# RWKV attention with a squared-ReLU FFN: half of the w_in loads issued on the ACT queue, with new order tables

## The chip, the cores and the metric

The kernel runs on one core of one Trainium2 chip. The metric is the device time of one execution in microseconds. Before the change three runs took 559.23, 558.83 and 562.87 us; the median is 559.23 us.

## The reference

The inputs have 4 sequences (batch), 8 heads, 768 positions and a head width of 48. First a linear recurrence with decay runs over the positions, then a two-layer FFN with a squared ReLU runs over all 3072 tokens, with 384 inputs and 2048 hidden units. All is float32.

```python
for t in range(S):                       # per sequence and head
    kt, vt, rt, wt = (k[:, :, t], v[:, :, t], r[:, :, t], w[:, :, t])
    cur = np.einsum('bhd,bhe->bhde', u[None] * kt, vt)
    y[:, :, t] = np.einsum('bhd,bhde->bhe', rt, state + cur)
    state = wt[:, :, :, None] * state + np.einsum('bhd,bhe->bhde', kt, vt)
x = y.transpose(0, 2, 1, 3).reshape(B * S, H * D)
h = np.maximum(x @ w_in, 0.0)
out = h * h @ w_out
```

## The kernel before

The 768 positions are cut into 6 chunks of 128. A chunk of one sequence is a "unit", so there are 24 units, four to a chunk. The recurrence inside a unit is done by matmuls.

**One unit** goes through these steps. SP loads w, k and r into a tile `st` (one transfer each, for one or for two sequences) and v into `v`. For chunk 0 TensorE transposes them (`turn`, line 399); later chunks use VectorE's stream transpose and small transfers (`z`, `pt`). VectorE forms the running product of w (`scan`, line 411), ACT takes its logarithm and an exponential of minus that (`ln`, lines 418 and 419), VectorE makes the scaled r and k (`rt`, `kn`, lines 422 to 431), TensorE multiplies them (`mt`, line 459), ACT builds the diagonal term (`diag`, line 448, eight small instructions in a unit), VectorE masks (`mask`, line 463), TensorE mixes in v (`mix`, lines 484 to 508), and ACT and VectorE write the result as a high and a low part into `x` (lines 525 and 526). ACT also runs a range check on w (`far`, lines 450 and 451).

**The weights** come in 8 groups g. The loads of `w_in` go to a tile `ri`, those of `w_out` to `ro`. A group of `w_in` is four transfers: for the lower half of the partitions one of 48 rows (288 KB) and one of 16 rows (96 KB), and the same for the upper half (`load_w`, line 305). A group of `w_out` is one transfer of 768 KB (line 307). Each group is then split into a high and a low part (`split_w`): ACT (line 318), VectorE three times (322, 326, 331), ACT (338), GpSimd (339).

**The FFN** runs in steps f = 0 to 15 for each chunk: nine matmuls into `hp` (line 573), ReLU and square by ACT and VectorE (578 to 582), then three matmuls for each sequence into `ob` (line 588). For the first 6 steps of chunk 0 and for all of chunk 1 a step is done for two sequences at a time (256 columns instead of 512).

**The order** of everything is set by a planner inside the kernel (`Plan`). Each step is added with an engine, a cost and a rank. The planner repeatedly takes the step that can start earliest by its own costs and, among equals, the one of lowest rank. The ranks come from tables: `AT` and `AT0` by the name of the step, `U0`, `C1`, `W0`, `WL` by unit or weight group, `OFF` and `LAG` for the FFN. The planner has two transfer queues, `"sp"` and `"actq"`; it keeps for each queue a time of its own at which its wire is free. A step of `"actq"` takes its place in the instruction order of ACT.

**Landing semaphores.** The transfers of both queues are numbered in program order and take eight landing semaphores (DMAHW0 to DMAHW7) in turn. A transfer is issued only once the transfer eight places before it has landed; its engine's queue stands still until then. Before the change only the load of `u` at the start and the last four stores are on the ACT queue; everything else is on SP.

Of the kernel before, what the change touches and what calls it, by code (L numbers as in the profile page):

```python
# [169 lines left out]

@with_exitstack
def kernel(
    ctx: ExitStack,
# [37 lines left out]
    wi_r, wi_t, wo_r, wo_t = [], [], [], []  # L213
# [10 lines left out]
    for i in range(3):  # L224
        g = place(f"g{i}", [128, 2, 512], F32R, None)
# [11 lines left out]
    far = const.tile([128, NC * B], F32, name="far")  # L237
# [17 lines left out]
    P = Plan()  # L255
# [42 lines left out]
    def load_w(g, rank):  # L298
        before = first_use(0) if g == NG - 1 else [s for s in P.steps if any(x.pool == "ly" for x in s.slots)] if g == NG - 2 else []

        pairs = w_in32[g, 0:KT * R].rearrange("(k p) x -> p k x", k=KT)
        for j in range(2):
            last = w_in32[g, KT * R + j * D:KT * R + j * D + D].rearrange("(k p) x -> p k x", k=KT)
            for i, (to, n, src) in enumerate(((j * J, D, pairs[j * D:j * D + D]), (j * J + D, J - D, last))):
                P.add("sp", 1.4 if n == D else 0.5, rank, lambda to=to, n=n, src=src: nc.sync.dma_start(out=wi_r[g][to:to + n], in_=src),
                      w=[("wi", g, j, i)], after=before if g == NG - 1 else [], runs=3 * n)
        P.add("sp", 2.4, rank, lambda: nc.sync.dma_start(out=wo_r[g], in_=w_out32[g]), w=[("wo", g, 0, 0)],
              after=before, runs=256)

    def split_w(g, rank):  # L310
        for nm, rt, tt, parts in (("wi", wi_r[g], wi_t[g], [("wi", g, j, i) for j in range(2) for i in range(2)]),
                                  ("wo", wo_r[g], wo_t[g], [("wo", g, 0, 0)])):
            bits = rt.rearrange("p k x -> p (k x)").rearrange("p (x z) -> p x z", z=2)
            q = Slot("q")
            raw, lead = (nm, g, "raw"), (nm, g, "lead")

            def widen(q=q, bits=bits):
                A.activation(q.tile, bits.bitcast(F32)[:, :, 1], AF.Copy, scale=2.0 ** -112)

            def shift(q=q):  # L320
                qi = q.tile.bitcast(U32)
                V.tensor_scalar(out=qi, in0=qi, scalar1=3, scalar2=None, op0=ALU.logical_shift_left)

            def sign(q=q, bits=bits):
                qi = q.tile.bitcast(U32)
                V.scalar_tensor_tensor(out=qi, in0=bits[:, :, 1], scalar=0x80000000, in1=qi,
                                       op0=ALU.bitwise_and, op1=ALU.bitwise_or)

            def low(q=q, bits=bits):
                qi = q.tile.bitcast(U32)  # L330
                V.scalar_tensor_tensor(out=qi, in0=bits[:, :, 0], scalar=29, in1=qi,
                                       op0=ALU.logical_shift_right, op1=ALU.bitwise_or)

            P.add("act", 0.8, rank, widen, r=parts, w=[q])
            P.add("dve", 0.48, rank, shift, w=[q], port=True)
            P.add("dve", 0.88, rank, sign, r=parts, w=[q], port=True)
            P.add("dve", 0.88, rank, low, r=parts, w=[q], port=True)
            P.add("act", 0.74, rank, lambda q=q, tt=tt: A.copy(out=tt[:, 0], in_=q.tile), r=[q], w=parts + [lead])
            P.add("pool", 1.9, rank, lambda q=q, tt=tt: G.tensor_tensor(out=tt[:, 1], in0=q.tile, in1=tt[:, 0].bitcast(F32), op=ALU.subtract),
                  r=[q, lead], w=[(nm, g, "rest")])  # L340
# [221 lines left out]
    def ffn(P, c, f, rank, bs=(0, B), s0=None):  # L562
        n = (bs[1] - bs[0]) * C
        xT = xTs[c if c == SLOW else c % 2]
        xs = slice(bs[0] * C, bs[1] * C)
        hp, g = Slot("hp"), Slot("g")
        wkeys = lambda nm: [(nm, f // 2, "lead"), (nm, f // 2, "rest")]

        def first():
            m = 0  # L570
            for kt in range(KT):
                for wl, xl in ((0, 0), (0, 1), (1, 0)):
                    T.matmul(hp.tile[:, 0:n], wi[f][:, wl, kt], xT[:, kt, xl, xs], start=(m == 0), stop=(m == 3 * KT - 1))  # L573
# [7 lines left out]
        P.add("act", 0.53 if full else 0.31, rank("g"), lambda: A.copy(out=hi(), in_=h()), r=[hp], w=[(g, 0)])  # L581
        P.add("dve", 0.61 if full else 0.33, rank("g"), lambda: V.tensor_tensor(out=lo(), in0=h(), in1=hi().bitcast(F32), op=ALU.subtract),  # L582
              r=[hp, (g, 0)], w=[(g, 1)])
        for b in range(*bs):
            def second(b=b):
                for m, (gl, wl) in enumerate(((0, 0), (0, 1), (1, 0))):
                    o = (b - bs[0]) * C
                    T.matmul(obs[b][:, 0:DM], g.tile[0][:, gl, o:o + C], wo[f][:, wl], start=(f == 0 and m == 0), stop=(f == NF - 1 and m == 2))  # L588
            P.add("pe", 0.525, rank("ob"), second, r=wkeys("wo") + [(g, 0), (g, 1)], w=[("ob", b)])
            if f == NF - 1:  # L590
                os_ = Slot("q")
                ob = out[b * S:b * S + S]
                P.add("act", 0.4, rank("os"), lambda b=b, os_=os_: A.copy(out=os_.tile[:, 0:DM], in_=obs[b][:, 0:DM]), r=[("ob", b)], w=[os_])  # L593
                q_, e = ("actq", nc.scalar) if c == NC - 1 else ("sp", nc.sync)
                P.add(q_, 1.1, rank("os"), lambda b=b, os_=os_, ob=ob, e=e: e.dma_start(out=ob[c * C:c * C + C] if s0 is None else ob[ds(s0, C)], in_=os_.tile[:, 0:DM]), r=[os_])


    AT = {"load": -12.5, "z": -10, "pt": -10.5, "rk": -7.0, "beta": -5.0, "far": 9.25, "v": -6.0, "scan": -2.25, "ln": 7.0, "rt": -6, "kn": 3.25, "diag": -3.5, "mt": 5, "mask": 3.25, "ktp": 5.25, "kt": 12.5, "mix": 4.25, "x": 1.5, "x3": -5.0, "send": 3.0, "dS": 3.5, "S": 1.25}
    AT0 = {"load": -13.0, "turn": -1.5, "rk": -2, "beta": 0.2, "far": 9.25, "v": -6.75, "scan": -1.75, "ln": 5.25, "rt": 0.25, "kn": 2, "diag": 9.5, "mt": -1.0, "mask": 3.75, "ktp": 7.25, "kt": -1, "mix": 3, "x": 7.75, "x3": -1, "send": 4.0, "dS": 7.5, "S": -4}
    U0 = (-16, -15.25, -6.75, -5.5)  # L600
    C1 = (5.25, 13, 34.5, 36)
    WL = (-8.25, -8, -9, -5.5, -1.75, -7, -8.25, -13.5)
    OFF = {"hp": -1.0, "g": -6.5, "ob": 0.75, "os": -7.5}
    W0 = (-12.5, -9.5, -1, 0.25, 0.25, 5.5, 5.0, 17)
    HALF = (6, 16, 0, 0, 0, 0)
    LAG = 2

    def rank_of(c, b):
        if c == 0:
            return lambda nm: U0[b] + AT0[nm]  # L610
        return lambda nm: (C1[b] if c == 1 else 8 * ((c - 1) * B + b) - 4) + AT[nm]

    for b in range(B):
        attention(0, b, rank_of(0, b))
    for g in range(NG):
        load_w(g, W0[g] + WL[g])
        split_w(g, W0[g])
    x = 0
    for c in range(NC):
        if c:  # L620
            for b in range(B):
                attention(c, b, rank_of(c, b))

        order = [(f, bs) for bs in ((0, 2), (2, B)) for f in range(HALF[c])] + [(f, (0, B)) for f in range(HALF[c], NF)]
        for f, bs in order:
            step = (bs[1] - bs[0]) / 2
            ffn(P, c, f, lambda nm, x=x, step=step: x + OFF[nm] + (LAG * step if nm in ("ob", "os") else 0), bs)
            x += step
    with tc.manual_schedule():
        P.run()  # L630
# [14 lines left out]
    with tc.If(any_bad > 0):  # L645
        with tc.tile_pool(name="dram", bufs=1, space=bass.MemoryType.DRAM) as dr, \
# [8 lines left out]
            with tc.For_i(0, S, TB) as t0:  # L655
# [8 lines left out]
                for t in range(TB):  # L664
                    rt, kt, wt = (tk[nm][:, t].unsqueeze(2).broadcast_to(sh) for nm in "rkw")
# [7 lines left out]
                for b in range(B):  # L673
                    nc.sync.dma_start(
                        out=xd[b * S:b * S + S].rearrange("s (h d) -> h s d", d=D)[:, ds(t0, TB)],
                        in_=ys[b * H:b * H + H])
            with tc.For_i(0, S, C) as s0:
# [17 lines left out]
                P = Plan()  # L695
# [36 lines left out]
```

## Time and profile before

| | |
|---|---|
| runs | 559.23, 558.83, 562.87 us, median 559.23 us |
| profiled execution, span from first to last instruction | 559.9 us (the page has no other time of this execution) |
| TensorE busy | 530.8 us (95%) |
| VectorE busy | 359.1 us (64%) |
| ScalarE (ACT) busy | 288.0 us (51%) |
| GpSimd busy | 101.3 us (18%) |
| transfers | 50.86 MB, mean 91 GB/s |

A row of the profile names the line, the engine, the operation and the tiles, with buffer numbers left out. "SPq" and "ACTq" rows are the issuing of transfers by SP and ACT; the time beside them is how long the issue held that queue, not how long the data took.

### The profile page before, as it was taken

How to read it: one execution, taken by the hardware profiler on the slowest of the kernel's cores; microseconds unless marked ns; L12 is line 12 of the kernel's file. 1: busy time of each engine (PE TensorE's matmuls, PEld its weight loads, DVE VectorE, ACT ScalarE, POOL GpSimd, SP SyncE). 2: the span in 40 equal slices, each digit the busy share in tenths (PEclk: the TensorE clock that was granted, in tenths of full speed). 3: DMA queues.
4: the chain of work that ended last, by engine and by line, in shares of the span. 5: the costliest groups of instructions: out<-in, count | busy, mean ns of one | idle time of the engine just before them, and what ended most of it. 6: DMA issues, size and time to landing. Idle time of an engine off the chain costs nothing. (4 is left out here: it accounts for less than half of the span.)

```text
span 559.9 us, 10076 instructions
## 1 busy us (share of the span) xinstructions
PE 530.8 (95%) x3800; PEld 466.7 (83%) x3800; DVE 359.1 (64%) x643; ACT 288.0 (51%) x677; POOL 101.3 (18%) x115
## 2 busy tenths in 40 slices
PE   4768898999999999999999999999999999999995
PEld 3557787889998999988888888888888888998994
DVE  5789879898759596776866767567475233332330
ACT  2786776668554747555554554553563222332322
POOL 4253552352203003030401102102000000000000
PEclk9998898999999999999999999999999999999999
DMA  9999699237472645637470470460440000010001
GB/s 156 210 240 217 122 255 218 39 64 137 99 141 51 111 109 91 123 78 135 80 132 2 78 168 24 84 129 2 78 106 3 12 1 1 14 58 2 0 1 60
DMA packets 206326, 50.86 MB, mean 91 GB/s; under 512 B 196032, under 2 KB 201152, under 8 KB 206272
## 3 DMA queue, kind: packets, MB, share of 16 engines
q1 hardware_dynamic: 205552, 49.17, 43.9%
q10 hardware_dynamic: 720, 0.98, 0.5%
q8 instruction: 32, 0.52, 0.4%
q14 instruction: 22, 0.18, 0.1%
HBM read 31.65 MB, written 4.72 MB: 65 GB/s over the span
## 5 line engine op out<-in xcount | busy, mean ns | idle before, releaser
L573 PE MATMUL hp<-x,wi 128*128 128x512 f32 (+1 forms) x1062 | 225.6, 358 | 4.7 <-DVE g L582 4.7
L588 PE MATMUL ob<-wo,g 128*128 128x384 f32 x1152 | 224.7, 341 | 4.4 <-ACT g L581 4.4
L588 PEld LDWEIGHTS ob<-wo,g 128*128 128x128 f32 x1152 | 200.5, 189 | 12.2 <-ACT g L581 4.9
L573 PEld LDWEIGHTS hp<-x,wi 128*128 128x128 f32 x1062 | 175.5, 190 | 31.9 <-DVE g L582 5.8
L579 DVE SCALAR_TENSOR_TENSOR hp<-hp,t 128x512 f32<-128x512 f32 (+1 forms) x118 | 70.2, 596 | 110.5 <-ACT t L578 110.0
L578 ACT ACTIVATE t<-hp 128x512 f32<-128x512 f32 (+1 forms) x118 | 60.9, 516 | 136.8 <-PE hp L573 111.2
L582 DVE TENSOR_TENSOR g<-hp,g 128x512 fp32r<-128x512 f32 (+1 forms) x118 | 69.1, 586 | 37.7 <-ACT g L581 35.9
L581 ACT CAST g<-hp 128x512 fp32r<-128x512 f32 (+1 forms) x118 | 59.2, 504 | 54.6 <-DVE hp L579 54.4
L448 ACT ACTIVATE m<-ident,beta 128x128 f32<-128x128 f32 x192 | 60.5, 395 | 7.0 <-DVE beta L441 7.0
L438 POOL TENSOR_TENSOR st<-st 128x384 f32<-128x384 f32 x24 | 25.1, 1047 | 64.7 <-DVE st L367 63.5
L463 DVE COPY_PREDICATED m<-caus,a 128x512 f32<-128x512 uint8 x48 | 33.0, 731 | 5.5 <-PE a L459 5.5
L459 PEld LDWEIGHTS a<-pt 48*128 48x128 f32 x384 | 25.8, 199 | 11.4 <-issue 7.1
L459 PE MATMUL a<-pt 48*128 48x128 f32 x384 | 30.8, 298 | 4.4 <-DVE pt L431 4.4
L526 DVE SCALAR_TENSOR_TENSOR x<-a,x 112x128 fp32r<-112x128 f32 (+2 forms) x44 | 17.9, 432 | 20.5 <-ACT x L525 19.9
L493 PE MATMUL a<-m,v 128*48 128x128 f32 (+1 forms) x384 | 28.5, 291 | 2.3 <-DVE m L463 1.8
L525 ACT ACTIVATE x<-a 112x128 fp32r<-112x128 f32 (+2 forms) x44 | 15.2, 389 | 28.8 <-PE a L493 28.5
L411 DVE TENSOR_TENSOR_SCAN pt<-pt,zero 112x128 f32<-112x128 f32 x80 | 28.9, 410 | 0.3 <-DMA x<-x 0.3
L493 PEld LDWEIGHTS a<-m,v 128*48 128x48 f32 (+1 forms) x384 | 21.4, 134 | 7.5 <-issue 4.5
L440 POOL TENSOR_TENSOR st<-st,un 128x384 f32<-128x384 f32 x24 | 26.9, 1120 | 1.6
L367 DVE STREAM_TRANSPOSE st<-st 128x1152 f32<-128x1152 f32 x20 | 26.8, 1359 | 0.0
L553 POOL TENSOR_TENSOR S<-S,Ec 112x192 f32<-112x192 f32 x16 | 8.2, 510 | 102.0 <-DVE S L552 102.0
L418 ACT ACTIVATE m<-pt 112x512 f32<-112x512 f32 x24 | 15.2, 635 | 20.1 <-DVE pt L411 15.7
(72 smaller groups left out, 394.5 us busy)
## 6 DMA issues: line engine op xcount, KB each, us to landing
pt<-st SPq DMA_DIRECT2D x80, 96.0 KB, 2.3
ro<-in_moe_w_out_dram SPq DMA_DIRECT2D x8, 768.0 KB, 9.6
v<-in_v_dram SPq DMA_DIRECT2D x24, 192.0 KB, 3.1
ri<-in_moe_w_in_dram SPq DMA_DIRECT2D x16, 288.0 KB, 9.1
st<-in_w_dram SPq DMA_DIRECT2D x11, 384.0 KB, 4.7
st<-in_k_dram SPq DMA_DIRECT2D x11, 384.0 KB, 5.3
st<-in_r_dram SPq DMA_DIRECT2D x11, 384.0 KB, 5.6
pt<-st SPq DMA_DIRECT2D x80, 48.0 KB, 2.5
```

The lines of the kernel that those rows point to most:

```text
L411: lambda p=p: V.tensor_tensor_scan(out=pt[:, 0, p], data0=src(0)[:, p], data1=zero.broadcast_to([HP, C]), initial=1.0, op0=ALU.mult, op1=A ...
L440: P.add("pool", 1.0, rank("rk"), lambda: G.tensor_tensor(out=rk(), in0=rk(), in1=un.rearrange("s (h d) -> s h d", d=D), op=ALU.mult), w=[( ...
L448: A.activation(mv(j)[:, p], ident, AF.Copy, scale=beta.tile[:, 2 * p + j:2 * p + j + 1])
L459: T.matmul(mts[j].tile.rearrange("s (p t) -> s p t", p=NP)[:, p], pt[js, 2, p], pt[js, 1, p], start=True, stop=True)
L463: lambda j=j: V.copy_predicated(out=mv(j), mask=caus.unsqueeze(1).broadcast_to([128, NP, C]), data=mts[j].tile.rearrange("s (p t) -> s p t ...
L493: T.matmul(ybv()[j * J:j * J + n_, p], vt.tile[:, o:o + n_], mv(j)[:, p], start=(c == 0 and p == KT), stop=True, skip_group_check=True)
L573: T.matmul(hp.tile[:, 0:n], wi[f][:, wl, kt], xT[:, kt, xl, xs], start=(m == 0), stop=(m == 3 * KT - 1))
L578: P.add("act", 0.5 if full else 0.28, rank("g"), lambda: A.activation(t(), h(), AF.Relu), r=[hp], w=[(g, 1)])
L579: P.add("dve", 0.61 if full else 0.33, rank("g"), lambda: V.scalar_tensor_tensor(out=h(), in0=h(), scalar=0.0, in1=t(), op0=ALU.max, op1=A ...
L581: P.add("act", 0.53 if full else 0.31, rank("g"), lambda: A.copy(out=hi(), in_=h()), r=[hp], w=[(g, 0)])
L582: P.add("dve", 0.61 if full else 0.33, rank("g"), lambda: V.tensor_tensor(out=lo(), in0=h(), in1=hi().bitcast(F32), op=ALU.subtract), r=[h ...
L588: T.matmul(obs[b][:, 0:DM], g.tile[0][:, gl, o:o + C], wo[f][:, wl], start=(f == 0 and m == 0), stop=(f == NF - 1 and m == 2))
```

## The change

The two transfers of each `w_in` group to the upper half of the partitions (j = 1) are issued on the ACT queue instead of SP. That is 16 transfers, 384 KB in each group. All rank tables have new numbers, and chunk 1 gets a table of its own (`AT1`) beside `AT0` for chunk 0 and `AT` for the later chunks. The split into half steps (`HALF`) stays. No computation is added or removed.

```diff
@@ load_w
-                P.add("sp", 1.4 if n == D else 0.5, rank, lambda to=to, n=n, src=src: nc.sync.dma_start(out=wi_r[g][to:to + n], in_=src),
+                q_, e = ("actq", nc.scalar) if j else ("sp", nc.sync)
+                P.add(q_, 1.4 if n == D else 0.5, rank, lambda to=to, n=n, src=src, e=e: e.dma_start(out=wi_r[g][to:to + n], in_=src),
                       w=[("wi", g, j, i)], after=before if g == NG - 1 else [], runs=3 * n)
@@ the tables (two of them)
-    U0 = (-16, -15.25, -6.75, -5.5)
-    W0 = (-12.5, -9.5, -1, 0.25, 0.25, 5.5, 5.0, 17)
+    U0 = (-48.5, -29.5, -19.25, 8)
+    W0 = (-73.25, -62.25, -28.25, 2, -3, 3, 5.75, 17.25)
...
-    for b in range(B):
-        attention(0, b, rank_of(0, b))
+    for b in range(B):
+        attention(0, b, lambda nm, b=b: RANKS.unit(0, b, nm))
```

What the tables do shows in the order of the instructions on each engine. A name with a number is a tile: `st_131` holds w, k, r of units 0 and 1, `st_132` those of units 2 and 3, `ri_56`, `ri_60`, `ri_64`, `ri_72`, `ri_80`, `ri_76`, `ri_68` are w_in groups 0, 1, 2, 4, 6, 5 and 3, `ro_58` is w_out group 0, and `m_150` and `m_151` hold the logarithms of units 0 and 1. Lines after the change are 34 or 35 higher.

ACT at the start of the program, before the change, with what each row waits for:

```order
L283 DMA un<-in_u_dram 128x384
L418 ACTIVATE m_150<-pt_123 112x512 [waits DVE_49,Pool_49]
L419 ACTIVATE m_150<-m_150 112x512 [waits Activation_49]
L421 COPY pt_123<-ob_136 112x4 [waits DVE_49]
L418 ACTIVATE m_151<-pt_123 112x512 [waits DVE_49]
```

ACT at the same place after the change, from the ninth transfer in its queue on (ahead of these rows stand the load of `u` and the upper halves of groups 0, 1 and 2):

```order
L340 DMA ri_72<-in_moe_w_in_dram 48x3x512 [waits DMAHW2_49]
L340 DMA ri_72<-in_moe_w_in_dram 16x3x512 [waits DMAHW4_49]
L340 DMA ri_80<-in_moe_w_in_dram 48x3x512 [waits DMAHW6_49]
L340 DMA ri_80<-in_moe_w_in_dram 16x3x512 [waits DMAHW0_49]
L453 ACTIVATE m_150<-pt_123 112x512 [waits DVE_49,Pool_49]
L340 DMA ri_76<-in_moe_w_in_dram 48x3x512 [waits DMAHW3_49]
L456 COPY pt_123<-ob_136 112x4 [waits DVE_49]
L454 ACTIVATE m_150<-m_150 112x512 [waits Activation_49]
L340 DMA ri_76<-in_moe_w_in_dram 16x3x512 [waits DMAHW5_49]
L340 DMA ri_68<-in_moe_w_in_dram 48x3x512 [waits DMAHW7_49]
L340 DMA ri_68<-in_moe_w_in_dram 16x3x512 [waits DMAHW1_49]
L453 ACTIVATE m_151<-pt_123 112x512 [waits DVE_49]
```

The logarithm of unit 0 was ACT's first arithmetic, behind one transfer; now ten transfers of w_in stand ahead of it, and fourteen ahead of the logarithm of unit 1.

SP at the start before the change, from the last load of `st_131` on:

```order
L358 DMA st_131<-in_r_dram 128x8x48
L387 DMA v_147<-in_v_dram 128x8x48
L387 DMA v_148<-in_v_dram 128x8x48 [waits DMAHW0_49]
L305 DMA ri_56<-in_moe_w_in_dram 48x3x512 [waits DMAHW1_49]
L305 DMA ri_56<-in_moe_w_in_dram 16x3x512 [waits DMAHW2_49]
L305 DMA ri_56<-in_moe_w_in_dram 48x3x512 [waits DMAHW3_49]
L305 DMA ri_56<-in_moe_w_in_dram 16x3x512 [waits DMAHW4_49]
L307 DMA ro_58<-in_moe_w_out_dram 128x2x768 [waits DMAHW5_49]
L358 DMA st_132<-in_w_dram 128x16x48 [waits DMAHW6_49]
```

SP after the change, from the same load on:

```order
L393 DMA st_131<-in_r_dram 128x8x48 [waits DMAHW0_49]
L393 DMA st_132<-in_w_dram 128x16x48 [waits DMAHW2_49]
L393 DMA st_132<-in_k_dram 128x16x48 [waits DMAHW4_49]
L393 DMA st_132<-in_r_dram 128x16x48 [waits DMAHW6_49]
L422 DMA v_147<-in_v_dram 128x8x48 [waits DMAHW0_49]
L340 DMA ri_56<-in_moe_w_in_dram 48x3x512 [waits DMAHW1_49]
L340 DMA ri_56<-in_moe_w_in_dram 16x3x512 [waits DMAHW3_49]
L342 DMA ro_58<-in_moe_w_out_dram 128x2x768 [waits DMAHW5_49]
L422 DMA v_148<-in_v_dram 128x8x48 [waits DMAHW7_49]
L340 DMA ri_60<-in_moe_w_in_dram 48x3x512 [waits DMAHW1_49]
```

The three large loads of `st_132` have moved ahead of v, of w_in group 0 and of w_out group 0.

The transfers of both queues in program order after the change, and the landing that each waits for (numbers are places in that order):

| place | queue, transfer | waits for the landing of |
|---|---|---|
| 0, 1, 4, 5, 7, 8 | SP, `st_131` (six loads of 192 KB) | 8 waits for 0 |
| 3, 6, 9, 11, 13, 15 | ACT, upper halves of groups 0, 1, 2 | from 9 on: 1, 3, 5, 7 |
| 10, 12, 14 | SP, `st_132` (three loads of 384 KB) | 2, 4, 6 |
| 16 | SP, `v_147` | 8 |
| 17, 19 | SP, `ri_56` lower half | 9, 11 |
| 18, 20, 22, 24 | ACT, upper halves of groups 4 and 6 | 10, 12, 14, 16 |
| 21, 23, 25 | SP, `ro_58`, `v_148`, `ri_60` lower (48 rows) | 13, 15, 17 |
| 27, 29, 31, 33 | ACT, upper halves of groups 5 and 3 | 19, 21, 23, 25 |

TensorE at the first FFN matmul (`hp`), before the change and then after it; both stand at the same place in TensorE's order, row 55:

```order
L399 MATMUL ob_138<-ident,st_132 128x128 x4
L471 MATMUL a_141<-ident,pt_123 128x112 x4
L573 MATMUL hp_140<-x_130,wi_57 128x256 x9
L399 MATMUL ob_138<-ident,st_132 128x128 x4
L544 MATMUL a_141<-v_148,m_152 64x48
```

```order
L434 MATMUL a_141<-ident,st_132 128x128 x4
L506 MATMUL a_142<-ident,pt_123 128x112 x4
L608 MATMUL hp_140<-x_130,wi_57 128x256 x9
L494 MATMUL a_141<-pt_124 128x128
L494 MATMUL a_142<-pt_124 128x128
```

Ahead of that matmul TensorE has nearly the same work in both; one group of four transposes has moved from behind it to ahead of it, and the scores of unit 2 (L494) have come up close behind it.

More of the change, by code (lines that the diff above doesn't have):

```diff
@@ L168, in run, with unit, load, split @@
             s.fn()
+class Ranks:
+    AT = {'load': 8.75, 'z': -1.75, 'pt': -108, 'rk': -122.75, 'beta': -59, 'far': 81, 'v': -8.75, 'scan': 11, 'ln': 9.25, 'rt': -111.75, 'kn': 96.75, 'diag': 67.75, 'mt': 55, 'mask': 1.25, 'ktp': 61.25, 'kt': -175.5, 'mix': -22.75, 'x': -16.25, 'x3': -50.5, 'send': -63.5, 'dS': -58.5, 'S': -130.75}
+    AT0 = {'load': -72.25, 'turn': 39.25, 'rk': 2.25, 'beta': -9.5, 'far': 12.25, 'v': -3.75, 'scan': -18.75, 'ln': -76.5, 'rt': -0.25, 'kn': 8, 'diag': 29.25, 'mt': -134.25, 'mask': -84.75, 'ktp': 54.75, 'kt': -64.75, 'mix': -74.25, 'x': -40.5, 'x3': -123.75, 'send': 37.25, 'dS': -89, 'S': -46.5}
+    AT1 = {'load': 23.5, 'z': -37.25, 'pt': 6.75, 'rk': -3, 'beta': -35.5, 'far': 61, 'v': -23, 'scan': -5.25, 'ln': 35, 'rt': -4.5, 'kn': 3.25, 'diag': 43, 'mt': -20.5, 'mask': -11.25, 'ktp': -11.75, 'kt': 47, 'mix': -19.25, 'x': 33.75, 'x3': -103.25, 'send': -42.75, 'dS': -67, 'S': -121.75}
+    U0 = (-48.5, -29.5, -19.25, 8)
+    C1 = (11.25, 12, 33, 55.5)
+    W0 = (-73.25, -62.25, -28.25, 2, -3, 3, 5.75, 17.25)
+    WL = (21.25, 39, 9, 39, -14.5, 22.75, 1.75, 28.25)
+    OFF = {'hp': -23.75, 'g': -8, 'ob': 140.5, 'os': -207.25}
+    LAG = 5.75
+    def unit(self, c, b, name):
+        if c == 0:
+            return self.U0[b] + self.AT0[name]
+        if c == 1:
+            return self.C1[b] + self.AT1[name]
+        return 32 * (c - 1) + 8 * b - 4 + self.AT[name]
+    def load(self, g):
+        return self.W0[g] + self.WL[g]
+    def split(self, g):
+        return self.W0[g]
+    def ffn(self, name, x, step):
+        return x + self.OFF[name] + (self.LAG * step if name in ("ob", "os") else 0)
+RANKS = Ranks()
+HALF = (6, 16, 0, 0, 0, 0)
 @with_exitstack
@@ L595, in ffn @@
                 P.add(q_, 1.1, rank("os"), lambda b=b, os_=os_, ob=ob, e=e: e.dma_start(out=ob[c * C:c * C + C] if s0 is None else ob[ds(s0, C)], in_=os_.tile[:, 0:DM]), r=[os_])
-    AT = {"load": -12.5, "z": -10, "pt": -10.5, "rk": -7.0, "beta": -5.0, "far": 9.25, "v": -6.0, "scan": -2.25, "ln": 7.0, "rt": -6, "kn": 3.25, "diag": -3.5, "mt": 5, "mask": 3.25, "ktp": 5.25, "kt": 12.5, "mix": 4.25, "x": 1.5, "x3": -5.0, "send": 3.0, "dS": 3.5, "S": 1.25}
-    AT0 = {"load": -13.0, "turn": -1.5, "rk": -2, "beta": 0.2, "far": 9.25, "v": -6.75, "scan": -1.75, "ln": 5.25, "rt": 0.25, "kn": 2, "diag": 9.5, "mt": -1.0, "mask": 3.75, "ktp": 7.25, "kt": -1, "mix": 3, "x": 7.75, "x3": -1, "send": 4.0, "dS": 7.5, "S": -4}
-    U0 = (-16, -15.25, -6.75, -5.5)
-    C1 = (5.25, 13, 34.5, 36)
-    WL = (-8.25, -8, -9, -5.5, -1.75, -7, -8.25, -13.5)
-    OFF = {"hp": -1.0, "g": -6.5, "ob": 0.75, "os": -7.5}
-    W0 = (-12.5, -9.5, -1, 0.25, 0.25, 5.5, 5.0, 17)
[L605 to L611, printed above, removed]
     for b in range(B):
-        attention(0, b, rank_of(0, b))
+        attention(0, b, lambda nm, b=b: RANKS.unit(0, b, nm))
     for g in range(NG):
-        load_w(g, W0[g] + WL[g])
-        split_w(g, W0[g])
+        load_w(g, RANKS.load(g))
+        split_w(g, RANKS.split(g))
     x = 0
@@ L621 @@
             for b in range(B):
-                attention(c, b, rank_of(c, b))
+                attention(c, b, lambda nm, c=c, b=b: RANKS.unit(c, b, nm))
         order = [(f, bs) for bs in ((0, 2), (2, B)) for f in range(HALF[c])] + [(f, (0, B)) for f in range(HALF[c], NF)]
@@ L626 @@
             step = (bs[1] - bs[0]) / 2
-            ffn(P, c, f, lambda nm, x=x, step=step: x + OFF[nm] + (LAG * step if nm in ("ob", "os") else 0), bs)
+            ffn(P, c, f, lambda nm, x=x, step=step: RANKS.ffn(nm, x, step), bs)
             x += step
```

## The prediction

> **What bounds the kernel now.** I read the page first, then the stretches that it suggests, then the waits of TensorE. The first three lines below are the page's; the last three are busy times in three stretches.
>
> ```profile
> span 559.9 us, 10076 instructions
> PE 530.8 (95%) x3800; PEld 466.7 (83%) x3800; DVE 359.1 (64%) x643; ACT 288.0 (51%) x677; POOL 101.3 (18%) x115
> PE   4768898999999999999999999999999999999995
> ...
> 0.00:32.65 32.65, 21.36 (x152) 16.37 (x153) 23.04 (x48) 17.37 (x41) 11.99 (x24) 1.00 1.12 195
> 32.65:98.00 65.35, 54.02 (x391) 47.41 (x389) 56.33 (x95) 46.37 (x109) 28.24 (x20) 0.92 0.94 206
> 98.00:553.40 455.40, 455.40 (x3263) 402.87 (x3262) 279.74 (x502) 223.29 (x527) 61.07 (x72) 1.00 0.33 66
> ```
>
> TensorE is the bound. From 98 us to its last matmul at 553.4 us it has no gap at all (455.40 busy in 455.40 us), with VectorE at 61% and ACT at 49%. All that an order can win or lose lies in the first 98 us, where TensorE stands idle for 32.65 - 21.36 = 11.3 us ahead of the first FFN matmul and 65.35 - 54.02 = 11.3 us between that and 98 us. In the second part VectorE is busy for 56.33 of 65.35 us, as full as TensorE. I cut at 32.65 us because there the first FFN matmul starts:
>
> ```profile
> 0.84 0.42 ACTq L283 DMA_DIRECT2D un<-in_u_dram  x1
> 8.45 0.63 ACT L418 ACTIVATE m<-pt 112x512 f32<-112x512 f32 x1 [6.36 <-DVE pt L411]
> 12.22 0.63 ACT L418 ACTIVATE m<-pt 112x512 f32<-112x512 f32 x1 [2.05 <-DVE pt L411]
> 29.70 0.49 ACT L525 ACTIVATE x<-a 128x384 fp32r<-128x384 f32 x1
> 32.65 1.31 PE L573 MATMUL hp<-x,wi 128*128 128x256 f32 x9
> ```
>
> These rows are the chain that opens the program: the logarithm of unit 0 at 8.45 us, that of unit 1 at 12.22 us, `x` of unit 1 at 29.70 us, the first FFN matmul at 32.65 us. The first half step of the FFN needs both units, so it stands 32.65 - 12.22 = 20.4 us behind the second logarithm. TensorE's own waits say the same of the rest:
>
> ```profile
> PE ob L399 <- DMA st<-in_w_dram: 5.9, 1, 5.9
> PE hp L573 <- DVE g L582: 4.7, 3, 2.0
> PE a L459 <- DVE pt L431: 4.4, 3, 2.5
> PE ob L588 <- ACT g L581: 4.4, 1, 4.4
> ```
>
> After the first load it waits for VectorE and ACT, never for a weight that has not landed.
>
> **The change: what ACT now waits for.** ACT executes in order. In the new order ten w_in transfers stand ahead of the logarithm of unit 0, and the last of them (place 24) may be issued only when `v_147` (place 16) has landed. That such waits hold a queue shows on SP before the change (who waited, for whose landing; total, times, longest):
>
> ```profile
> SPq L305 <- DMA ro<-in_moe_w_out_dram: 4.0, 1, 4.0
> SPq L305 <- DMA ri<-in_moe_w_in_dram: 2.3, 3, 1.0
> ```
>
> *When v_147 lands.* Before, the two v loads are the seventh and eighth of 192 KB on SP, and the second one is issued at 8.7 us and lands at most 5.2 us later, at 13.9 us (second row: times to landing).
>
> ```profile
> L387 SPq DMA_DIRECT2D v<-in_v_dram x2: 1135/1139/1143, 7.6 to 8.7; - x2
> DMA to landing us min/median/max: 5.0/5.1/5.2
> ...
> 7.00:9.80 2.80, 2.64 (x10) 1.84 (x11) 1.87 (x5) 1.26 (x2) 0.65 (x2) 1.00 1.38 170
> 19.00:24.00 5.00, 4.06 (x28) 3.34 (x30) 4.64 (x8) 4.38 (x13) 0.00 (x0) 1.00 1.55 166
> 31.00:33.00 2.00, 2.00 (x31) 1.95 (x28) 1.78 (x6) 1.65 (x3) 1.43 (x1) 1.00 1.13 298
> 53.00:60.00 7.00, 5.36 (x56) 4.02 (x56) 5.93 (x7) 2.65 (x5) 5.22 (x4) 0.76 1.07 190
> 75.00:77.00 2.00, 0.95 (x8) 0.92 (x8) 1.51 (x4) 1.83 (x7) 2.00 (x1) 1.00 1.02 389
> ```
>
> In the rows by stretch the last number is GB/s. After the change `v_147` is the thirteenth unit of 192 KB on SP (six for `st_131`, six for the three double loads of `st_132`, one for itself). Loads of this kind alone move at 166 to 170 GB/s (rows 7 to 9.8 and 19 to 24), so a unit of 0.197 MB takes 1.17 us, and five more make 13.9 + 5.9 = 19.8 us if the ACT queue's transfers cost nothing. Ahead of that landing ACT has sent the upper halves of groups 0, 1 and 2, 1.18 MB; if they stand in line at the 190 GB/s of w_in (row 53 to 60) that is 6.2 us more, 26.0 us. Where both kinds of packet move together the row 31 to 33 shows 298 GB/s, so most of it rides beside: I take 21 us, nearer the lower end. Against 8.45 us before, the first logarithm is 12.5 us late.
>
> *When unit 1 may start.* Four more ACT transfers stand ahead of the second logarithm, the last waiting for the lower half of group 1 (place 25). Between `v_147` and that, SP moves 0.295 + 0.098 (group 0), 0.786 (w_out), 0.197 (v) and 0.295 = 1.67 MB, and ACT up to 1.08 MB (places 18, 20, 22, 24, 27). Before, one whole w_in group and one w_out block, 1.57 MB, landed between 13.9 us and 12.53 + 7.1 = 19.6 us:
>
> ```profile
> 12.53 0.43 SPq L307 DMA_DIRECT2D ro<-in_moe_w_out_dram  x1
> ro<-in_moe_w_out_dram SPq DMA_DIRECT2D x1, 768.0 KB, 7.1
> ```
>
> That is 275 GB/s, so 6.1 us for SP's part alone and 10.0 us for both; I take 8. The second logarithm then starts at 29 us (bounds 25.9 and 36.0) instead of 12.22.
>
> *From there to the first FFN matmul.* In the new order ACT has between the second logarithm and `x` of unit 1: six logarithms and exponentials, 24 diagonal instructions, two range checks and small copies, the copies and reads of the w_in and w_out split, one `x`.
>
> ```profile
> L448 ACT ACTIVATE m<-ident,beta 128x128 f32<-128x128 f32 x32 | 10.1, 390 | 0.7 <-DVE beta L441 0.7
> L419 ACT ACTIVATE m<-m 112x512 f32<-112x512 f32 x4 | 2.5, 633 | 0.0
> L451 ACT ACTIVATE st<-st,nfar 128x384 f32<-128x384 f32 x4 | 2.5, 613 | 0.0
> L450 ACT ACTIVATE st<-st,nmid 128x384 f32<-128x384 f32 x4 | 2.4, 601 | 0.0
> L318 ACT ACTIVATE q<-ri x8: 889/896/939, 18.2 to 107.7; 128x768 f32<-128x768 f32 x8
> L338 ACT CAST wi<-q 128x768 fp32r<-128x768 f32 x3 | 2.5, 828 | 3.6 <-DVE q L331 3.6
> L511 ACT COPY ly<-a 112x128 f32<-112x128 f32 x4 | 1.1, 266 | 1.3 <-PE a L493 0.7 <-DVE q L331 0.6
> L473 ACT COPY m<-a 128x448 f32<-128x448 f32 x2 | 1.1, 526 | 0.0
> ```
>
> By these: 6 x 0.63 = 3.8; 24 x 10.1 / 32 = 7.6; two checks at 0.60 + 0.61 and 0.4 of reads and copies each, 3.2; two reads of 0.9, 1.8; 0.83 for the CAST, 2 x 0.27 and 0.53 for copies, 0.49 for `x`; 0.42 for one more transfer issue (row of `u`). Sum 19.2 us. With `x` of unit 1 and its low part on VectorE, some 1.1 us, it is again the 20.4 us of before. So the first FFN matmul comes at 29 + 20.4 = 49.4 us, **16.8 us later** (bounds 13.7 and 23.8). TensorE's work ahead of it has not grown by more than four transposes, so this is idle time.
>
> *What comes back.* By then ACT and VectorE have done some 2.3 us more than before (the diagonal terms and an exponential of units 2 and 3 on ACT, two steps of `kn` and two sums on VectorE, less one step of w_out's split). More weights lie ready, too. The gaps behind the first FFN matmul, 11.3 us, are the most that can come back; the least is the 2.3 us scaled by 65.35 / 56.33, 2.7 us. Since those gaps end on VectorE and ACT (the waits above) and not on loads, I take 6.
>
> *The rest.* SP loses 16 issues, which nobody waited for. ACT gains 16 at 0.42 us, 6.7 us; they are hidden beyond the first stretch, since ACT is busy for 46.37 of 65.35 us there. Behind 98 us the order changes with VectorE and ACT as cover; I cost it at 0, at most 4.4 us (one more wait like the last of TensorE's rows) if that cover fails; there is no gap that could shrink.
>
> **Sum** against the profiled execution: 559.9 + 16.8 - 6 = 570.7 us. The median of the runs is 0.7 us below the span, so **570 us**. Bounds: 559.9 + 13.7 - 11.3 = 562.3 and 559.9 + 23.8 - 2.7 + 4.4 = 585.4.
>
> A rule stands beside the choice of 21 us. The Trainium skill, "DMA: Bandwidth & Descriptors", section "Rules for kernel authors", says of two transfers to disjoint halves of the partitions not to bother, since they serialize on the same engines. By it the upper end, 26.0 us, would hold; but w_in halves move at 190 GB/s here and whole w_out blocks at 389 (row 75 to 77), which leaves room, so I give the rule less weight than the rows.
>
> **The rivals.**
> *The two queues share one wire.* Then `v_147` lands at 26 us and place 25 ten us later, the first FFN matmul is 23.8 us late, and with 6 us back the time is 577. For it: packets of `st` already keep all 16 engines busy (share above 1 in rows 7 to 24). Against it: 298 GB/s in the mixed stretch. Chance 0.15. This is the outcome that the rule of the Trainium skill gives.
> *The delay is nearly all given back.* The front is limited by VectorE's total work, which does not grow; with weights at hand its 56.33 us run without a gap: 13.7 - 11.3 = 2.4 us, 562. The new order also starts TensorE's transposes of units 2 and 3 sooner. Against it: VectorE stands behind ACT's exponential of unit 0 and then of unit 1, idle. Chance 0.20.
> *Faster: both halves land together and the loads run at full rate.* At 389 GB/s (row 75 to 77) the 6.5 MB up to place 25 take 16.7 us; counted from the first issue near 0.8 us the second logarithm starts at 17.5 us, the first FFN matmul is 5.3 us late, the 11.3 us of later gaps close, and the clock, granted at 0.92 in that stretch, comes back to 1.00 (54.02 x 0.08 = 4.3 us): 559.9 + 5.3 - 11.3 - 4.3 = 549.6. It is faster by over 1% if place 25 lands before 22 us. The loads of `st`, 2.4 of the 6.5 MB, move at 166 to 170 GB/s in the rows above, which speaks against it. Chance 0.14.
> The forecast itself, 565.5 to 575, keeps 0.51.
>
> **How the numbers follow.** A difference of 1% (5.6 us) is about what runs of this kernel can tell from none. Faster by over 1%: 0.13. Within 1%: 0.21, the case given back and the edge of the forecast. Slower: 0.66, the forecast and the shared wire. The range leaves out most of the faster case and the last few us below the upper bound, together under 2 in 10: 554 to 581.
>
> **What would show it.** In the new profile the first logarithm (line 453) should start near 21 us and the second near 29, each behind an ACTq row of w_in that waits for a landing; the first FFN matmul (line 608) near 49 us; TensorE's idle time up to then near 28 us instead of 11.3, with VectorE idle in the same place; and no gap worth a microsecond after some 110 us. A first logarithm before 15 us would make the argument wrong at its root; one at 21 us with an FFN start before 40 us would make the chain of 20.4 us wrong; new gaps in the middle of the program would put the cost where I have not looked.

## The result, and the profile after

Four runs of the changed kernel took 585.64 to 588.18 us, median **587.84 us**; the kernel before, run beside it on the same chip, 559.05 us. The ratio is 1.048 (95% interval 1.045 to 1.052): 4.8% slower. I had forecast 570 us and a range of 554 to 581. The sign was right, the size was not.

The first fence is from the page of the changed kernel (span, busy times, TensorE by slices), the second gives busy times in three stretches: up to the first FFN matmul, as long a stretch again, and the rest. Its columns are the stretch and its length, the busy time of TensorE, of its weight loads, of VectorE, ACT and GpSimd (with counts), TensorE's granted clock as a share of the full one, the busy share of the DMA engines, and GB/s.

```profile
span 586.5 us, 10062 instructions
PE 528.4 (90%) x3800; PEld 463.5 (79%) x3800; DVE 358.1 (61%) x643; ACT 289.9 (49%) x677; POOL 104.3 (18%) x115
PE   2106888999999999999999999999999999999995
```

```profile
0.00:66.61 66.61, 21.36 (x157) 16.72 (x157) 25.89 (x53) 21.70 (x56) 15.51 (x28) 0.68 1.01 172
66.61:132.00 65.39, 59.68 (x429) 51.37 (x428) 59.49 (x96) 47.77 (x100) 31.94 (x18) 0.98 0.67 140
132.00:580.00 448.00, 447.16 (x3219) 395.44 (x3217) 272.70 (x496) 219.36 (x520) 56.83 (x69) 1.00 0.33 66
```

Ahead of the first FFN matmul TensorE is busy for 21.36 us, to the digit what it was before. But this stretch now lasts 66.61 us instead of 32.65. Idle time there has grown from 11.3 to 45.25 us; in the next 65 us it fell from 11.3 to 5.7; behind that TensorE has next to no gap (0.8 us in 448).

The chain that opens the program, from the timeline of ACT and of TensorE (start, duration; in brackets the idle time before and what ended it):

```profile
1.30 31.56 ACTq L340 DMA_DIRECT2D ri<-in_moe_w_in_dram  x10
32.96 0.63 ACT L453 ACTIVATE m<-pt 112x512 f32<-112x512 f32 x1 [30.86 <-DMA ri<-in_moe_w_in_dram]
39.03 4.85 ACTq L340 DMA_DIRECT2D ri<-in_moe_w_in_dram  x3
43.93 0.63 ACT L453 ACTIVATE m<-pt 112x512 f32<-112x512 f32 x1 [7.89 <-DMA ri<-in_moe_w_in_dram]
...
46.08 2.08 PE L494 MATMUL a<-pt 48*128 48x128 f32 x16 [27.33 <-DVE pt L466]
66.61 2.27 PE L608 MATMUL hp<-x,wi 128*128 128x256 f32 x9
```

ACT's queue is held by the ten w_in transfers until 32.86 us; the logarithm of unit 0 follows at 32.96 (8.45 before), that of unit 1 at 43.93 (12.22 before). TensorE names VectorE as what it waits for, but VectorE waits for ACT, and ACT for a landing.

Why that landing is late shows on SP in the same kernel (how long each issue held SP's queue; last row: the times of the first three v loads to landing):

```profile
1.96 3.43 SPq L393 DMA_DIRECT2D st<-in_r_dram  x1
...
12.31 4.93 SPq L393 DMA_DIRECT2D st<-in_k_dram  x1
17.28 4.89 SPq L393 DMA_DIRECT2D st<-in_r_dram  x1
22.22 2.62 SPq L422 DMA_DIRECT2D v<-in_v_dram  x1
...
DMA to landing us min/median/max: 10.3/12.0/14.5
```

Some of SP's own issues are held for 3 to 5 us, the first of these rows although it waits for no landing, so it is not landings alone that hold them. SP comes to `v_147` at 22.22 us (7.6 us before the change), and the load lands 10.3 us later, at 32.5, which lets ACT's tenth transfer go; its issue ends at 32.86. The rate between 2 and 28 us, after and before (last number, GB/s):

```profile
2.00:28.00 26.00, 6.04 (x24) 4.00 (x24) 3.78 (x12) 0.10 (x1) 3.89 (x8) 0.80 1.20 161
```

```profile
2.00:28.00 26.00, 16.89 (x96) 12.55 (x98) 18.12 (x37) 12.97 (x35) 8.72 (x12) 1.00 1.22 197
```

With two queues at work and another mix of loads less arrives than before, 161 against 197 GB/s. Which of the two lowers it is tested below, with w_in among the loads of st from one queue.

### The profile page after: what moved, and what is told of

The parts are those of the page before. It is cut to its first block, busy times and chain, and to the rows that moved or that the text cites. A ratio compares the mean times of both kernels' runs of the same rounds, so it can differ in the third digit from the quotient of the medians.

```text
span 586.5 us, 10062 instructions
## 1 busy us (share of the span) xinstructions
PE 528.4 (90%) x3800; PEld 463.5 (79%) x3800; DVE 358.1 (61%) x643; ACT 289.9 (49%) x677; POOL 104.3 (18%) x115
## 5 line engine op out<-in xcount | busy, mean ns | idle before, releaser
L608 PE MATMUL hp<-x,wi 128*128 128x512 f32 (+1 forms) x1062 | 221.3, 357 | 3.7 <-DVE g L617 3.5
L623 PE MATMUL ob<-wo,g 128*128 128x384 f32 x1152 | 221.6, 339 | 1.4 <-DVE g L617 1.0
L608 PEld LDWEIGHTS hp<-x,wi 128*128 128x128 f32 x1062 | 173.7, 190 | 33.9 <-DVE g L617 6.2
L494 PE MATMUL a<-pt 48*128 48x128 f32 x384 | 30.6, 298 | 27.6 <-DVE pt L466 27.6
L494 PEld LDWEIGHTS a<-pt 48*128 48x128 f32 x384 | 25.7, 198 | 34.4 <-ACT m L454 27.7
L453 ACT ACTIVATE m<-pt 112x512 f32<-112x512 f32 x24 | 15.1, 630 | 45.4 <-DMA ri<-in_moe_w_in_dram 38.8
L446 DVE TENSOR_TENSOR_SCAN pt<-pt,zero 112x128 f32<-112x128 f32 x80 | 30.4, 423 | 1.3 <-DMA x<-x 0.9
L463 DVE TENSOR_TENSOR pt<-pt,m 112x512 f32<-112x512 f32 x24 | 16.3, 682 | 23.9 <-ACT m L454 23.9
L528 PE MATMUL a<-m,v 128*48 128x128 f32 (+1 forms) x384 | 27.5, 283 | 0.3 <-DVE m L498 0.3
L402 DVE STREAM_TRANSPOSE st<-st 128x1152 f32<-128x1152 f32 x20 | 26.6, 1355 | 0.0
L462 POOL COPY Ec<-pt 112x4 f32<-112x4 f32 x20 | 9.0, 455 | 98.9 <-DVE pt L446 70.0
L475 POOL TENSOR_TENSOR st<-st,un 128x384 f32<-128x384 f32 x24 | 25.5, 1063 | 1.5
```

Of the source, the lines that this page charges most:

```text
L402: V.transpose(out=zt[:, i].rearrange("a t p q i -> a t (p q) i"), in_=sv[:, :, i].rearrange("s t p q x -> s t (p q) x"))
L446: lambda p=p: V.tensor_tensor_scan(out=pt[:, 0, p], data0=src(0)[:, p], data1=zero.broadcast_to([HP, C]), initial=1.0, op0=ALU.mult, op1=A ...
L494: T.matmul(mts[j].tile.rearrange("s (p t) -> s p t", p=NP)[:, p], pt[js, 2, p], pt[js, 1, p], start=True, stop=True)
L528: T.matmul(ybv()[j * J:j * J + n_, p], vt.tile[:, o:o + n_], mv(j)[:, p], start=(c == 0 and p == KT), stop=True, skip_group_check=True)
```

## The experiments

I held three theories against each other: (1) ACT's arithmetic stands behind issues that wait; (2) the bytes of w_in now travel ahead of what the engines need first, whatever queue issues them; (3) the order that the new tables give the engines is itself poorer. Ratios are against the kernel before, run on the same chip, with 95% intervals. `Log 1` and `log 2` are the logarithms of units 0 and 1, FFN is the first FFN matmul.

| kernel | median us | ratio | log 1, log 2, FFN at us |
|---|---|---|---|
| before | 559.05 to 561.83 | 1 | 8.45, 12.22, 32.65 |
| changed | 587.84 | 1.048 (1.045 to 1.052) | 32.96, 43.93, 66.61 |
| changed order, halves from SP | 574.94 | 1.026 (1.022 to 1.031) | 9.37, 21.02, 52.77 |
| changed order, halves from GpSimd | 574.3 | 1.023 (1.019 to 1.027) | 8.43, 19.29, 52.51 |
| changed order, both halves together on SP | 563.79 | 1.006 (1.004 to 1.008) | 8.47, 13.31, 37.91 |
| ACT halves behind the exponentials | 582.3 | 1.037 (1.033 to 1.042) | 8.55, 12.23, 45.48 |
| the same order, halves from SP | 571.79 | 1.018 (1.014 to 1.022) | 8.50, 12.17, 40.07 |
| six ahead on ACT | 577.38 | 1.028 (1.023 to 1.033) | 15.12, 18.50, 50.41 |
| group 0 alone on ACT, new tables | 577.37 | 1.027 (1.023 to 1.032) | 10.29, 16.10, 38.53 |
| v first, fourteen ahead on ACT | 611.29 | 1.089 (1.085 to 1.094) | 33.78, 37.16, 60.59 |
| old tables, halves planned on ACT | 604.56 | 1.078 (1.074 to 1.083) | 24.66, 42.09, 61.73 |
| old order, halves from ACT | 571.11 | 1.018 (1.012 to 1.024) | 8.47, 12.21, 34.59 |
| old order, halves from GpSimd | 562.35 | 1.003 (1.000 to 1.006) | 8.38, 12.21, 32.97 |
| old order, group 0 alone from ACT | 560.58 | 1.001 (0.998 to 1.004) | 8.44, 12.24, 32.62 |

**The changed order with another issuer.** The planner still places the upper halves as steps of ACT; only the engine that issues them differs, so every arithmetic instruction keeps its place.

```diff
-                q_, e = ("actq", nc.scalar) if j else ("sp", nc.sync)
+                q_, e = ("actq", nc.sync) if j else ("sp", nc.sync)
```

> The changed program in its own order, every instruction at its place, but the 16 upper halves of w_in are issued by SP instead of ACT. Theory 1 (ACT's arithmetic stands behind issues that wait for landings): the first logarithm comes back to 8 to 11 us from 32.96, and most of the 28 us goes: 559 to 570. Theory 2 (what is late is the data: the order brings 2.75 MB of w_in ahead of v, whatever queue issues it): the logarithm is early, but the first FFN matmul still stands beyond 50 us, and the time stays at 575 to 588. Theory 3 (the new tables are a poorer order for the engines even with the loads at hand): 580 to 588 with an early FFN start and gaps later on.

Timeline and rate of this kernel:

```profile
9.37 0.63 ACT L453 ACTIVATE m<-pt 112x512 f32<-112x512 f32 x1 [7.27 <-DVE pt L446]
21.02 0.63 ACT L453 ACTIVATE m<-pt 112x512 f32<-112x512 f32 x1 [4.34 <-DVE pt L446]
...
45.59 0.67 PE L528 MATMUL a<-m,v 128*64 128x128 f32 x4 [0.93 <-DMA v<-in_v_dram]
52.77 1.31 PE L608 MATMUL hp<-x,wi 128*128 128x256 f32 x9
...
2.00:28.00 26.00, 8.72 (x41) 6.16 (x41) 9.91 (x22) 5.71 (x17) 6.14 (x11) 1.00 1.19 157
```

The first logarithm is back at 9.4 us, and 12.9 of the 28.8 us are gone. The rest stays, with the first FFN matmul at 52.8 us: unit 1's w and the loads of v come in behind w_in. So neither theory 1 nor theory 2 holds alone, and 574.9 lies just under the range that I gave for theory 2.

With `nc.gpsimd` in the same line:

> The changed program in its own order, with the upper halves of w_in issued by GpSimd: two queues again, but ACT is free; GpSimd's own steps (the sel mask, u, the sums of the diagonal term) stand behind its issues instead. Theory 2 (one wire: the bytes ahead of v count, however many queues): as with SP alone, first logarithm at 8 to 11 us, first FFN matmul at 50 to 58, 570 to 580. Rival (two queues at once are worse than one with the same bytes): first FFN matmul beyond 60 us, 580 or more.

```profile
2.00:28.00 26.00, 8.63 (x40) 6.11 (x40) 9.38 (x24) 6.38 (x18) 15.04 (x25) 1.00 1.15 163
```

The same time as from SP alone, within its interval, and the same FFN start (52.51 us). One queue (SP) moved 157 GB/s, SP and GpSimd 163, SP and ACT 161: how many queues there are hardly matters to the rate. So the loss to ACT as issuer is ACT's own standing still.

**The changed order with both halves at the lower half's place**, issued by SP one behind the other (`up` is the upper half's target and source). Again every instruction of the engines keeps its place; what goes is w_in ahead of unit 1's loads and of v.

```diff
-                q_, e = ("actq", nc.scalar) if j else ("sp", nc.sync)
-                P.add(q_, ..., e.dma_start(out=wi_r[g][to:to + n], in_=src),
+                P.add("actq" if j else "sp", ..., None if j else (nc.sync.dma_start(out=wi_r[g][to:to + n], in_=src), nc.sync.dma_start(out=up[0], in_=up[1])),
```

> The changed program with every instruction of the five engines at its place, but both halves of a w_in group are issued by SP, one behind the other, at the place of the lower half. So ACT issues no w_in, and no w_in stands ahead of the first loads of v on SP. Of the 26.6 us that the changed kernel lost in its span, SP or GpSimd as issuer of the same transfers at the same places gave back 14; this tells what the other 12 are. Theory 2 (the bytes of w_in ahead of v and of w_in group 0's lower half): first logarithm at 8 to 10 us, second at 12 to 14, first FFN matmul at 32 to 38, 555 to 563 us. Theory 3 (the engines' order that the new tables make is itself poorer): the same early start, but 567 or more, with gaps behind 60 us that end on VectorE or ACT.

```profile
8.47 0.63 ACT L453 ACTIVATE m<-pt 112x512 f32<-112x512 f32 x1 [6.37 <-DVE pt L446]
13.31 0.63 ACT L453 ACTIVATE m<-pt 112x512 f32<-112x512 f32 x1 [2.62 <-DVE pt L446]
...
8.77 2.33 SPq L393 DMA_DIRECT2D st<-in_k_dram  x1
11.14 2.33 SPq L393 DMA_DIRECT2D st<-in_r_dram  x1
13.51 2.51 SPq L422 DMA_DIRECT2D v<-in_v_dram  x1
...
37.91 1.32 PE L608 MATMUL hp<-x,wi 128*128 128x256 f32 x9
...
2.00:28.00 26.00, 15.63 (x79) 11.46 (x81) 18.00 (x40) 12.06 (x35) 10.21 (x16) 1.00 1.19 198
```

563.8 us, 0.6% above the kernel before. The rate is back at 198 GB/s, and the two double loads of st hold SP for 2.33 us each instead of 4.9. This kernel also tests the base of my estimate: SP sends the same thirteen units of 192 KB, and ACT sends no w_in. `v_147` lands 6.6 us after the start of its issue, at 20.1 us; I had put 19.8 if the ACT queue's transfers cost nothing.

These kernels share one order of the engines, so the spans divide the 26.6 us: 586.5 - 572.0 = **14.5 for ACT as issuer**, 572.0 - 561.3 = **10.7 for w_in ahead of unit 1's loads and v**, 561.3 - 559.9 = 1.4 for the engines' order. Each span is one execution; the medians give 12.9, 11.2 and 2.8. The parts are those of this sequence of changes; in another sequence they could differ.

**ACT kept free until both exponentials are through.** The ACT queue stays, its transfers depend on the exponentials of units 0 and 1.

```diff
-                       w=[("wi", g, j, i)], after=before if g == NG - 1 else [], runs=3 * n)
+                       w=[("wi", g, j, i)], after=(before if g == NG - 1 else []) + (exps[0:2] if j else []), runs=3 * n)
```

> The changed kernel, in which the upper halves of w_in on the ACT queue come only after the exponentials of units 0 and 1. The ACT queue and the tables stay. Theory 1 and theory 2 both give back nearly all, since neither ACT nor the wire is taken ahead of the second logarithm: first logarithm at 8 to 10 us, second at 12 to 15, first FFN matmul at 32 to 38, time 556 to 565. Theory 3: 575 or more. Rival (two queues at once slow the loads wherever they fall): first logarithm early, but the first FFN matmul at 42 or later and 568 to 576.

```profile
16.54 7.27 ACTq L340 DMA_DIRECT2D ri<-in_moe_w_in_dram  x2
23.85 2.45 ACT L483 ACTIVATE m<-ident,beta 128x128 f32<-128x128 f32 x8 [8.38 <-DMA ri<-in_moe_w_in_dram]
...
66.49 7.44 ACTq L340 DMA_DIRECT2D ri<-in_moe_w_in_dram  x2
73.97 0.38 ACT L613 ACTIVATE t<-hp 128x256 f32<-128x256 f32 x1 [7.27 <-DMA st<-in_r_dram]
```

A miss: 582.3, not 556 to 565. The logarithms came early as said, but the block moved on: the diagonal terms of unit 0 and, at 66 us, the ReLU of the FFN stood behind two holds of over 7 us. It also gives a price for w_in beside the loads of st and v. SP issues `v_147` at 13.51 us as in the kernel with both halves together, but from 13.6 us on ACT issues three transfers of w_in, 0.69 MB, beside it, and the hold that ends with the landing of `v_147` lasts until 16.54 + 7.27 = 23.8 us. The landing itself is at 23.5 us instead of 20.1.

The same order with `nc.sync` as issuer:

> The order of the kernel before this one that put the upper halves of w_in behind the exponentials of units 0 and 1 (582.3 us, first FFN matmul at 45.5 us, two holds of 7.3 and 7.4 us on ACT), rebuilt so that SP issues them; ACT then waits for no landing. Theory 1 (ACT's arithmetic behind issues that wait is the cost): the first FFN matmul at 32 to 38 us, no stretch between 56 and 84 us in which TensorE is at 8 of 14 us, 558 to 567. Theory 3 (the new tables are a poorer order): 572 or more with gaps that end on VectorE or ACT. Theory 2 (loads late whatever queue issues them) says 562 to 570, since here the loads of v stand ahead of most of w_in.

```profile
27.43 0.89 ACT L353 ACTIVATE q<-ri 128x768 f32<-128x768 f32 x1 [2.49 <-DMA ri<-in_moe_w_in_dram]
```

The holds are gone, and 10.5 us with them, but 571.8 is above the 558 to 567 expected. Now ACT waits at its own read of w_in group 0. That read stands ahead of unit 0's copies as it did before the change (at 18.17 us there), but here its data comes in behind the large loads of `st_132`. TensorE waits 3.9 us for a load of v.

**How many stand ahead.** Groups 0, 1 and 2 ahead on ACT, the others behind the exponentials (`if j and g >= 3` in the line above):

> The changed kernel in which groups 0, 1 and 2 stay ahead of the first logarithm on ACT (six transfers) and the later groups come behind the exponentials of units 0 and 1. The sixth transfer waits for place 7, the fifth load of st_131. If the first logarithm starts when the landing comes for which the last issue ahead of it waits, it is at 11 to 15 us here, against 33 with ten ahead and 8.6 with none; the first FFN matmul at 40 to 52 and 566 to 580. If something else in the changed kernel held ACT, it would stay beyond 20 us.

```profile
1.30 13.72 ACTq L340 DMA_DIRECT2D ri<-in_moe_w_in_dram  x6
15.12 0.63 ACT L453 ACTIVATE m<-pt 112x512 f32<-112x512 f32 x1 [13.02 <-DMA ri<-in_moe_w_in_dram]
```

None ahead 8.6 us, six 15.1, ten 33.0: the logarithm starts when the last issue ahead of it is let go.

Only group 0's halves on ACT, which wait for nothing (`if j and g == 0`), the others planned on SP:

> The changed kernel with only the two upper transfers of w_in group 0 on the ACT queue, neither of which waits for a landing; the other fourteen are planned on SP. Tables stay. Theories 1 and 2: first logarithm at 9 to 11 us, first FFN matmul at 33 to 38, 557 to 566. Theory 3 (tables): 570 or more.

```profile
98.00:112.00 14.00, 8.10 (x30) 6.61 (x30) 9.59 (x15) 8.94 (x14) 6.97 (x4) 0.88 0.49 91
```

The early part came as theories 1 and 2 say (FFN at 38.5 us), the time as theory 3 says. The planner made a different order, with 5.9 us of idle TensorE at 98 to 112 us where the changed kernel has 0.9. The same tables cost 1.4 us of span in the changed kernel's own order, but kernels that the planner rebuilt from them with ACT free of holds stood 10 and 16 us above the one before (571.79 and 577.37); such a kernel tests two things at once.

**v first.** The rank of v in chunk 0 from -3.75 to -300:

> The changed kernel with the loads of v put first on SP (the rank of v in chunk 0 is -300). In the rebuilt order fourteen w_in transfers stand ahead of the first logarithm on ACT, the last behind place 25, another w_in transfer. If v had been the trouble (its landing is what the tenth issue waited for): first logarithm before 20 us and 560 to 570. If it is the bytes ahead of whatever the last issue waits for: some 5.3 to 6 MB at 161 GB/s, so the first logarithm at 35 to 39 us, the second at most 5 us behind it, the first FFN matmul at 56 to 64 us and 576 to 588.

```profile
33.78 0.63 ACT L453 ACTIVATE m<-pt 112x512 f32<-112x512 f32 x1 [31.68 <-DMA ri<-in_moe_w_in_dram]
37.16 0.63 ACT L453 ACTIVATE m<-pt 112x512 f32<-112x512 f32 x1 [2.04 <-DVE pt L446]
...
101.67 2.07 PE L494 MATMUL a<-pt 48*128 48x128 f32 x14 [15.95 <-DVE pt L466]
```

Fourteen ahead, the last waiting for a w_in transfer: 33.8 us, a little under the 35 to 39 from the bytes, and nowhere near 20. It was not v as such. The total, 611, is outside my 576 to 588: the rebuilt order has a second hole of 15.95 us, in which VectorE works mostly through the split of weights ahead of what TensorE waits for.

**The old tables.** First with the halves planned on ACT, then in the old order with every instruction at its place and only the issuer changed, `e=(nc.scalar if j else nc.sync)`:

> The kernel before with its own tables, and the upper halves of w_in planned on the ACT queue. Ten of these transfers stand ahead of the first logarithm, as in the changed kernel; v is ahead of the three large loads. Theories 1 and 2 (ACT's block, or the w_in traffic ahead): 575 to 590, the first logarithm beyond 25 us. Theory 3 (the tables): 557 to 562.

```profile
24.66 0.63 ACT L419 ACTIVATE m<-pt 112x512 f32<-112x512 f32 x1 [22.56 <-DMA ri<-in_moe_w_in_dram]
42.09 0.63 ACT L419 ACTIVATE m<-pt 112x512 f32<-112x512 f32 x1 [7.69 <-DMA ri<-in_moe_w_in_dram]
```

The block without the new tables, and 604.6 us, more than I had said.

> The kernel before in its own order, every instruction at its place, but the upper halves of w_in are issued by ACT instead of SP. Only one of them (group 0, 48 rows) stands ahead of the first logarithm's exponential, and it waits for the small load of u; the next waits for a load of unit 1. Theory 1: what counts is what an issue on ACT waits for, so the first logarithm stays at 8 to 10 us and the time at 556 to 563. Rival (any transfer on the ACT queue beside SP slows the loads or ACT): 567 or more.

```profile
37.27 0.63 ACT L419 ACTIVATE m<-m 112x512 f32<-112x512 f32 x1 [3.22 <-DMA ro<-in_moe_w_out_dram]
```

A miss: 571.1, not 556 to 563. The first logarithms were in time, as said, but later issues held ACT, here for 3.2 us. Then GpSimd in the same place (`nc.gpsimd`), and ACT for group 0 alone (`if j and g == 0`):

> The kernel before in its own order, with the upper halves of w_in issued by GpSimd, where the same with ACT took 571.1 us. If what cost 11 us there is that ACT's arithmetic stands behind issues that wait (theory 1), GpSimd, busy for 18% of the span, hides them: 557 to 564 us, first FFN matmul at 32 to 34 us. If a second queue by itself disturbs the loads: 567 or more again.

> The kernel before in its own order, with only the two upper transfers of w_in group 0 issued by ACT; both wait for loads that land early (u, and w of unit 1). Theory 1 (only an issue that waits while ACT has arithmetic due costs anything): 557 to 563 us. Rival (any use of the ACT queue costs some us, as the 571.1 us with all groups might be read): 565 or more.

Both as theory 1 says: 562.4 and 560.6 us, within 1% of the kernel before. Sixteen transfers on a second queue cost next to nothing from GpSimd (0.3%) and 10 us from ACT; two from ACT whose waits are over cost nothing. Neither gained anything. Three orders, each run with ACT and with another issuer, now price ACT as issuer: 587.8 to 574.9 or 574.3, 582.3 to 571.8, 571.1 to 562.4, that is 9 to 14 us. Not all of it need be standing still: TensorE's busy time is also shorter without ACT as issuer, by 3.9 us in the second order (537.4 to 533.5) and by 1.8 in the third (532.8 to 531.0); in the first it is not (528.4 to 531.6).

## Why the prediction was right or wrong

*The bound, and where it would be lost:* right. TensorE's work ahead of the FFN is 21.36 us in both kernels, and all the loss is idle time there. No gap of a microsecond came up behind some 110 us.

*The block on ACT:* right as a mechanism, tenth and fourteenth transfer included. The steps by size:

| step of the sum | predicted us | measured us |
|---|---|---|
| first logarithm, at the landing of v_147 | 21 (19.8 to 26.0) | 32.96 |
| from there to the second | 8 (6.1 to 10.0) | 10.97 |
| from there to the first FFN matmul | 20.4 | 22.68 |
| first FFN matmul later by | 16.8 (13.7 to 23.8) | 33.96 |
| given back | 6 (2.7 to 11.3) | 7.4 |

*The step that failed* is the landing of `v_147`, and in it the price of the w_in that ACT sends beside the loads of SP: 12 of the 16 us that the sum lacked. The base of the step was right: without w_in from ACT, `v_147` lands at 20.1 us (both halves together, above), against my 19.8. For w_in I added 1.2 us; it cost 12.4, 20.1 to 32.5. Three things were wrong in that price:

- The bytes. I counted 1.18 MB of w_in ahead of the landing, groups 0 to 2. But places 18, 20 and 22 wait only for loads of `st_132`, which land before v, so group 4 and most of group 6 were issued as well: 1.87 MB, of which 1.57 had moved when `v_147` landed.
- The rate. I let w_in ride beside the st loads, by the 298 GB/s of a stretch in which two thirds of the bytes were w_out and w_in. Beside the short rows of st it did not: all of it together came at 161 GB/s, below the 170 of st alone. The 2.56 MB of st and v and the 1.87 of w_in, 4.43 MB, take 27.5 us at that rate; from 2 us on that makes 29.5, within 3 us of the landing. What had in fact moved by the landing, with the load of `u` and 0.70 MB that SP sent behind v, is 2.56 + 1.57 + 0.20 + 0.70 = 5.03 MB, or 165 GB/s. Standing in line at 190 GB/s, my other price, the 1.87 MB would have cost 9.8 us.
- SP's issues. They are themselves held longer with ACT's transfers beside them: 4.93 and 4.89 us for two double loads, against 2.33 each in the kernel with both halves together. With that SP came to `v_147` at 22.2 us instead of 13.5.

*The second logarithm* came 3 us later behind the first than I had said, for a like reason: 223 GB/s arrived between the two, where I had taken 275 and let part of ACT's bytes ride beside. *The chain of 20.4 us* took 2.3 more. ACT was busy for 19.1 us of it, as my sum of 19.2 says, and TensorE for 15.3 us, as before the change (15.28 and 15.32), although its granted clock was 0.65 instead of 1.00. So the 2.3 us are waiting; on what was not separated. *Given back:* 6 against 7.4, near enough: 5.6 us of gaps and 2.4 of matmul time, less 0.8 of new gaps late on.

*The rival of one shared wire* had the mechanism that I gave 0.15: the bytes add up whatever queue they come from. The rule that I named there (the Trainium skill, "DMA: Bandwidth & Descriptors", "Rules for kernel authors": two transfers to disjoint partition halves serialize) agrees with 157, 161 and 163 GB/s from one queue and two, and with 562.4 and 560.6 us where the second queue cost nothing and brought nothing. I gave it too little weight, and its price, 577 us, still had the bytes too low, since it put the landing of `v_147` at 26 us. *Faster, at full rate* is refuted by the same rates. *Nearly all given back* failed because the delay, 34 us, was three times what there was to give back.

## What to carry to other kernels

A transfer that must wait for a landing is a barrier for all arithmetic behind it on the engine that issues it: put it on an engine with nothing due, or only where the wait is already over. Sum the bytes of all queues ahead of the first thing that an engine needs, at the rate measured for just that mix; in these runs a second queue shared the rate and added none. And to price one part of such a change, keep the order of the program and change the issuer alone, since a planner given one new rule makes another program.

## What was not expected of the hardware

TensorE's granted clock fell to half in the early stretches of some kernels. Two rows, of the changed kernel and of the old tables planned on ACT (third number from the right: the clock):

```profile
28.00:42.00 14.00, 0.00 (x0) 0.00 (x0) 3.72 (x7) 1.32 (x3) 2.46 (x3) 0.50 1.09 206
```

```profile
20.00:30.00 10.00, 0.00 (x0) 0.00 (x0) 0.00 (x0) 0.63 (x1) 0.00 (x0) 1.00 1.14 223
```

In the changed kernel TensorE stands idle at 0.50, and its first nine FFN matmuls then take 2.27 us where they took 1.31 from SP. But in the second kernel the clock is shown as 1.00 through 24 us without a matmul (20 to 44 us), and as 0.50 later, at 84 to 90 us, when it is busy for 5.19 of 6 us. Nor is it the ACT queue: the order rebuilt for SP alone has 0.59 from 14 to 42 us. What sets it in these rows stays open.
